# A fused layer norm, attention and gated MLP block: small steps moved from VectorE to GpSimd and the DMAs, and VectorE's exponentials taken in batches of eight

## The chip, the cores and the metric

The kernel runs on one core of one Trainium2 chip. A core has five engines, each with its own queue of instructions that it works off in order: TensorE (PE, matmuls into the PSUM memory), VectorE (DVE), ScalarE (ACT), GpSimd (POOL), and SyncE (SP), which here only issues DMAs. Engines wait for one another through semaphores. The metric is the device time of one execution in microseconds (us).

## The reference

Input x has 2,048 rows of 512. It is layer-normed, goes through attention with 32 heads of 16 that share one key and one value head, and through an MLP; the attention's output is multiplied by the silu of the MLP's output, and x is added. Cut to what matters:

```python
xn = _layernorm(x)                       # (x - m) / sqrt(v + 1e-5), rows of 512
q = (xn @ wq) as 32 heads of 16;  k = xn @ wk;  v = xn @ wv      # one k and v for all heads
p = softmax(q @ k.T * 16 ** -0.5)        # 32 x 2048 x 2048
s = (p @ v, heads side by side) @ wo
g = silu(silu(xn @ w1) @ w2)             # 512 -> 1792 -> 512
return x + s * g
```

## The kernel before

The program is written by a planner: Python code that keeps a clock for each engine, puts tasks with a cost, a priority, what they read and write and what must come first on a list per engine, and places them one by one on the engine whose clock is lowest. What comes out is a fixed order of instructions on every engine and the semaphore waits between them (`finalize`, `run_engine`). The constants at the top of the file are the costs and the rules of that order. On the chip nothing is reordered: an instruction whose input is late holds all behind it on its engine.

**Start.** x is loaded in tiles of 128 rows. For each tile VectorE takes mean and variance (lines 499 and 503), and for a group of two or four tiles the inverse root of the variance plus 1e-5 by a bit trick and two Newton steps: eight VectorE instructions on 128x2 or 128x4 numbers (lines 516 to 525), each waiting for the one before. `first = (2, 2, 4, 4, 4)` says how many tiles each group has. Then VectorE normalises the tiles (528), TensorE transposes them, and k and v are made. GpSimd clears parts of the key and value buffers in this stage (459, 461) and issues four DMAs; line 456 has it run one tiny INT64_ADD at the very start.

**Attention.** The 32 heads in four blocks of 512 rows make 32 groups `g`; two groups, `2*oi` and `2*oi + 1`, are one pair `oi`. A group has 64 slots, each a 128x512 block of scores that four matmuls write into one PSUM bank (line 898). A slot is turned into exponentials in one of two ways:

- by ScalarE's exponential, one bank or two neighbours at a time (line 1605), and then needs one product with v;
- by VectorE, which scales the scores into 16-bit integers whose bits, read as bf16, are near the exponential (line 974, into `db_sb`). Four such slots are a batch. For a batch GpSimd adds a constant to all its integers, three times with another constant (INT64_ADD, four 16-bit numbers a word, 128 x 512 words, line 1160, into `ds_sb`). The four versions, weighted in v, together are close enough to the exponential. Such a slot needs four products with v.

`pick_d` opens a batch and fills it slot by slot, `make_shifts` and `split` hand a full batch to GpSimd (`split` also puts the same work on VectorE's list, for the end of the run), and the step that starts slots (`s_step`) weighs the two ways by how much work waits for ScalarE and for VectorE. All products with v of a group add up in one bank (line 1238): 16 rows of results and 16 rows of their denominators for each quarter of 32 partitions.

**Closing a group** (`make_norm`). VectorE transposes the bank in place in 32x32 blocks (1255), takes the reciprocal of the denominators (1258) and multiplies (1260) into `otr_sb`, after which the bank is free. When both groups of a pair are done, VectorE transposes `otr_sb` into `on_sb` (1270), which the output projection reads.

**MLP and end.** Between the slots TensorE runs the MLP's products (665), ScalarE and VectorE its activations (713, 714). When four pairs of a block are closed, the output projection (`mk_w`) runs for its four row tiles, and `final` does the rest on VectorE: the product with the gate in PSUM (766) and the sum with x, which SP has loaded into `xr_sb`, into `ob_sb` (769); SP stores it (761). The last block has a tail of its own.

GpSimd and VectorE share a rule in the planner: a task with `ports=2` waits for the last such task of the other of the two engines. The shifts on GpSimd are such tasks; the evictions of line 974 are not.

Of the kernel before, what the change touches and what calls it, by code (L numbers as in the profile page):

```python
# [15 lines left out]
P = 128  # L16
# [3 lines left out]
W1_AT, SKIP = 5, 1500.0  # L20
T_ISSUE, T_SWDGE = 450.0, 1000.0
J_BASE, J_END, MIXJ = 0.073, 1.084, 3
# [4 lines left out]
T_P, T_SH, T_TR, T_AF = 600.0, 600.0, 630.0, 63.5  # L27
T_P64, DV_MIN, T_LIB = 1015.0, 40, 300.0
HOLD_PO = 374.374
RSQRT_M = float(0x5F1FFFF9)  # L30
RSQRT_C = ((-0.703952253, 0.703952253 * 2.38924456), (-0.5, 1.5))

Q_URG = 0.308
J_SLIP = 1.308
NEXT_OB, OB_SLACK = 6, 192.595
NORM_PRIO, T_DIV = 0, 264.0
A_OPEN = 5
T_MS, V_AT = 500.0, 7
# [10 lines left out]
LINE, FETCH, FED, LOOK = 256, 3684.358, 58, 68  # L49
# [3 lines left out]
NPA, NDB, NDS, NTM = 21, 5, 8, 4  # L53
MARGIN, MARGIN_END = 19, 20
WIDE, PAIR_WAIT, GRP_WAIT = 14, 47.267, 237.034
Q_LEAD = 4.233
A_HIGH, D_HIGH, SLACK = 1582.599, 1518.392, 43.301
LEAD, CROWD, FRAG, DB_LOW = 468.141, 0.617, 2.417, 1
RUN, HOLD, PRESS = 6, 1411.229, 18
ROOM = 5  # L60
START_Z, START_H, AHEAD, NEAR = 8, 9, 1.03, 17
CLOSING, URGENT, END_DV = 2, 4.336, 55
STARVED = 511.14
JLATE, JEVAC = 1.311, 1
# [250 lines left out]
def bass_recurrent_scan__grouped_kv_mqa__dense_activation_silu__prompt_kernel(  # L315
# [29 lines left out]
    with ExitStack() as es:  # L345
# [3 lines left out]
        xn_sb = sb("xn_sb", [P, 4, D], BF16)  # L349
# [14 lines left out]
        db_sb = sb("db_sb", [P, NDB, 4 * NQ], U16)  # L364
        ds_sb = sb("ds_sb", [P, NDS, 4 * NQ], U16)
        f_sb = sb("f_sb", [P, 2, NQ], FP32)
        rcp_sb = sb("rcp_sb", [P, 2, NQ // 32], FP32)
        otr_sb = sb("otr_sb", [P, 2, NQ], BF16)
# [5 lines left out]
        ob_sb = sb("ob_sb", [P, 4, D], BF16)  # L374
# [4 lines left out]
        var_sb = sb("var_sb", [P, 2, NT], FP32)  # L379
# [7 lines left out]
        zer_sb = ob_sb[:, 3, :]  # L387
# [3 lines left out]
        XB = NDS - 4  # L391

        def x_tile(t):
            return ds_sb[:, XB + t // 4, (t % 4) * NQ:(t % 4 + 1) * NQ].bitcast(BF16)

# [17 lines left out]
        def xkey(t):  # L413
            return ("Ds", XB + t // 4, t % 4)

        def ds_keys(s):
            return [("Ds", s, h) for h in range(4)]
# [6 lines left out]
        for j in range(1, 4):  # L424
            dma(SP, "x", ds_sb[:, XB + j, :].bitcast(BF16).rearrange("p (t d) -> p t d", d=D),
                xv[:, 4 * j:4 * j + 4, :], 512, ds_keys(XB + j), prio=1)
# [15 lines left out]
        pl.add(Task(DV, 550.0, lambda v: v.memset(zer_sb, 0.0), (), [("ob", 3)], 0))  # L442
# [9 lines left out]
        for j in range(K + 1):  # L452
            pl.add(Task(DV, 60.0, lambda v, j=j: v.memset(wj_sb[:, j:j + 1], 1.0 if j == 0 else SHIFT_W[j - 1]),
                        (), [("wj", j)], 2))
        l0 = pl.add(Task(PO, 60.0, lambda g: g.memset(lib_sb[:], 0), (), ["lib"], -2))
# [14 lines left out]
        for e in (1, 0):  # L470
# [16 lines left out]
        m1 = pl.add(Task(AC, 700.0, lambda a: a.activation(f_sb[:, 0, :], x_tile(1), ACT.Copy, scale=1.0 / D,  # L487
                                                          accum_out=mv_sb[:, 1, 0:1]),
                         [xkey(1)], [("F", 0), ("me", 1)], 0, gate=lambda: "scr2" in pl.lastw))
        m2 = pl.add(Task(AC, 210.0, lambda a: a.activation(scr_sb[:, 2:3], mv_sb[:, 1, 0:1], ACT.Copy, scale=-ISD),  # L490
                         [("me", 1)], ["nb"], 0, [m1]))
        pl.add(Task(AC, 700.0, lambda a: a.activation(f_sb[:, 0, :], x_tile(1), ACT.Square, scale=ISD, bias=scr_sb[:, 2:3],
                                                      accum_out=mv_sb[:, 1, 1:2]),
                    [xkey(1), "nb", ("me", 1)], [("F", 0), ("mv", 1)], 0, [m2]))
# [11 lines left out]
        first = (2, 2, 4, 4, 4)  # L506
        a = 0
        for n in first:
            b = a + n
            tiles = range(a, b)  # L510
            g = a // 4
            y, w, h = rstd_sb[:, a:b], var_sb[:, 0, a:b], var_sb[:, 1, a:b]

            def dv(fn, reads, writes, pre, ports=1):
                return pl.add(Task(DV, 66.0, fn, reads, writes, g, [pre] if pre is not None else [], ports=ports))
            t = pl.add(Task(DV, 66.0, lambda v, a=a, b=b, w=w: v.tensor_scalar(
                w, mv_sb[:, a:b, 1], LN_EPS, None, op0=ALU.add), [("mv", i) for i in tiles], [("ve", a)], g,
                [aggr[i] for i in tiles], ports=2))
            t = dv(lambda v, y=y, w=w: v.tensor_scalar(
                y.bitcast(I32), w.bitcast(I32), -0.5, RSQRT_M, op0=ALU.mult, op1=ALU.add), [("ve", a)], [("rs", a)], t, 2)  # L520
            for it, (c0, c1) in enumerate(RSQRT_C):
                t = dv(lambda v, y=y, h=h, c0=c0: v.scalar_tensor_tensor(  # L522
                    out=h, in0=y, scalar=c0, in1=y, op0=ALU.mult, op1=ALU.mult), [("rs", a)], [("vh", a)], t)
                t = dv(lambda v, w=w, h=h: v.tensor_tensor(h, h, w, ALU.mult), [("ve", a), ("vh", a)], [("vh", a)], t)  # L524
                t = dv(lambda v, y=y, h=h, c1=c1: v.scalar_tensor_tensor(
                    out=y, in0=h, scalar=c1, in1=y, op0=ALU.add, op1=ALU.mult), [("rs", a), ("vh", a)], [("rs", a)], t)
            for i in tiles:
                xn_task[i] = pl.add(Task(DV, 323.0, lambda v, i=i: v.tensor_scalar(  # L528
                    xn_sb[:, i % 4, :], x_tile(i), mv_sb[:, i, 0:1], rstd_sb[:, i:i + 1],
                    op0=ALU.subtract, op1=ALU.mult),  # L530
                    [xkey(i), ("rs", a), ("mv", i)], [("xn", i % 4)], 1 + g, [t], ports=2,
                    gate=lambda i=i: i < 4 or i - 4 in t_done))
            a = b
# [24 lines left out]
        def mk_T(tiles, bk=None):  # L558
            n, t0 = len(tiles), tiles[0]

            def rnd(b):
                def emit(pe, b=b):
                    dst = bank(b).bitcast(BF16).rearrange("p (t d) -> p t d", d=D)
                    h = None
                    for k, t in enumerate(tiles):
                        for dc in range(NDC):
                            h = pe.transpose(dst[:, k, dc * P:(dc + 1) * P], xn_sb[:, t % 4, dc * P:(dc + 1) * P], ident[:, :])
                    return h
                return emit
# [177 lines left out]
        def scaled(tt, b, r=None):  # L747
            k = tt % 2
            if r in EVR:
                ev = pl.add(Task(AC, 490.0, lambda a: a.activation(xn_sb[:, r, :], bank(b), ACT.Copy, scale=0.25),  # L750
                                 [("ps", b)], [("xn", r)], 0))
                fin_task[tt] = Task(DV, 333.0, lambda v: v.tensor_tensor(fin_sb[:, k, :], xn_sb[:, r, :], tmp_sb[:, tt % NTM, :], ALU.mult),
# [7 lines left out]
        def store(tt, t2):  # L760
            return pl.add(Task(SP, 60.0, lambda e: e.dma_start(of.rearrange("(t p) d -> p t d", p=P)[:, tt, :], ob_sb[:, tt % 4, :]),
                               [("ob", tt % 4)], [("out", tt)], 0, [t2], dma=128 * 1024, on_place=outs.append))

        def final(tt, b):
            k = tt % 2
            t1 = Task(DV, T_P, lambda v: v.scalar_tensor_tensor(
                out=bank(b), in0=bank(b), scalar=0.25, in1=tmp_sb[:, tt % NTM, :], op0=ALU.mult, op1=ALU.mult),
                [("ps", b), ("tmp", tt % NTM)], [("ps", b)], 0, [tmp_task[tt]])
            t2 = Task(DV, T_P, lambda v: v.tensor_tensor(ob_sb[:, tt % 4, :], bank(b), xr_sb[:, tt % 4, :], ALU.add),
                      [("ps", b), ("xr", tt % 4)], [("ob", tt % 4)], 0, [t1, xr_task[tt], out_task.get(tt - 4)])  # L770
# [5 lines left out]
        def add_xr(tt):  # L776
            xr_task[tt] = pl.add(Task(SP, 60.0, lambda e: e.dma_start(xr_sb[:, tt % 4, :], xv[:, tt, :]),
                                      (), [("xr", tt % 4)], 2, [fin_task[tt - 4]] if tt >= 4 else [], dma=128 * 1024))
# [3 lines left out]
        def mk_w(tt, pace):  # L782
            c, r = divmod(tt, 4)

            def consume(jb, op):
                t1, t2 = final(tt, jb.bank)
                if tt + 4 < NT:
                    add_xr(tt + 4)
                return [t1, t2]
# [151 lines left out]
        def pick_d(t):  # L941
            if st["assigned"] < 8 or any(k not in evac_kt or evac_kt[k].op is None for k in range(NKT)):
                return None
            for bt in batches:
                for k in range(4):
                    if k not in bt.slots and slot_time(bt.g, k % 2) <= t + 20:
                        return bt, k
            if any(len(bt.slots) < 4 for bt in batches):
                return None
            g = st["gD"]  # L950
            while g < NG and (nleft[g] < (MARGIN if g < NG - 1 else MARGIN_END) or min(len(left[g, i]) for i in range(2)) < 2):
# [7 lines left out]
            for k in range(2):  # L959
                if slot_time(g, k) <= t + 20:  # L960
                    bt = Job()
                    bt.g, bt.slots, bt.b, bt.P, bt.nsh, bt.left = g, {}, free[0], {}, 0, 4 * K
# [76 lines left out]
        def start_d(t, b, d):  # L1039
            bt, k = d  # L1040
            g, i = bt.g, k % 2
            if not bt.slots:
                batches.append(bt)
                db_busy[bt.b] = 1
                resv[g, 0], resv[g, 1] = 2, 2
# [63 lines left out]
        def make_shifts():  # L1109
            for bt in list(batches):  # L1110
                if len(bt.slots) < 4:
                    continue
                while bt.nsh < K - 1:
# [4 lines left out]
                    ds_busy[s] = 4  # L1118
# [10 lines left out]
        def split(bt, s, j):  # L1129
# [9 lines left out]
            def placed_dv(pop):  # L1139
# [3 lines left out]
                ready(pop, range(4))  # L1143

            def placed_po(pop):
# [4 lines left out]
                ready(pop, range(4))  # L1150

            reads = [("Db", bt.b, i) for i in range(4)]
# [93 lines left out]

        def make_norm(g):
            oi, e = divmod(g, 2)
            o3 = otr_sb[:, oi % 2, :].rearrange("p (b d) -> p b d", d=32)
# [3 lines left out]
            for h in range(parts):  # L1253
# [9 lines left out]
                    [("ps", OB), ("ps", OB, h), ("rcp", e, h)], [("otr", oi % 2, e, h)] + [("otr", oi % 2, e)] * (h == 0), NORM_PRIO,  # L1263
# [3 lines left out]
                if e == 0:  # L1267
# [3 lines left out]
                    on_sb[:, oi % NON, cols], otr_sb[:, oi % 2, cols]),  # L1271
# [209 lines left out]
        def do_tail(t, it):  # L1481
            if it[0] == "s":
# [5 lines left out]
                if part:  # L1488
                    t2 = pl.add(Task(AC, 490.0, lambda a: a.activation(ob_sb[:, tt % 4, :], bank(tb[4 + r]), ACT.Copy),
                                     [("ps", tb[4 + r])], [("ob", tt % 4)], 0, [out_task.get(tt - 4)]))  # L1490
# [17 lines left out]
        def pe_step():  # L1508
# [44 lines left out]
            if not t_done and ("ob", 3) in pl.lastw and pl.ready(PE, [("ob", 3)], [("ps", 6)]) <= t:  # L1553
                n = st["warm"] = st.get("warm", 0) + 1
                pl.tensor("F", None, T_COLD if n <= N_COLD else MM, lambda pe: pe.matmul(
                    bank(6), lhsT=zer_sb[:, 0:P], rhs=zer_sb[:, :], start=True, stop=True), [("ob", 3)], [("ps", 6)], t, n=2)
# [156 lines left out]
```

## Time and profile before

| | us |
|---|---|
| three runs | 676.65, 680.1, 683.86 (median 680.1) |
| the profiled execution | 674.7, its span 672.9 |
| TensorE / VectorE / ScalarE / GpSimd busy | 660.8 / 632.6 / 653.9 / 612.1 |
| first shift on GpSimd starts, last one ends | 43.8, 656.0 |

The span runs from the first to the last instruction; 1.8 us of the profiled execution lie outside it. Engines go by PE, DVE, ACT, POOL and SP; PEld is TensorE's loading of weights, which runs beside its matmuls; DMA-issuing instructions show as SPq or POOLq and are not counted as busy. A group's line names the source line, engine, operation, the tile written and the tile read, the shapes, the count, then busy time and the mean ns of one, and after the second bar the idle time of the engine just before these instructions and what ended it. A window's line gives start and end, length, and for each engine the busy us and the number of instructions; the last three columns are TensorE's granted clock (1.00 throughout), the busy share of the DMA engines and GB/s.

### The profile page before, as it was taken

To read this page: it belongs to the slowest core of one execution; us is meant where nothing else is said; L and a number is where in the kernel's file an instruction comes from. 1 tells how busy PE (TensorE), PEld (TensorE's weight loads), DVE (VectorE), ACT (ScalarE), POOL (GpSimd) and SP (SyncE) were. 2 spreads that over 40 slices of the span, in tenths; PEclk is the share of its full clock that TensorE was granted. 3 is DMA by queue.
4 is the path that set the end of the run, shared out by engine and by line. 5 is a ranking of instruction groups with operands and counts; after the bars stand their busy time and mean duration, and the time that the engine had idled before them with its cause. 6 is when DMAs were issued, how large, how long until landed. Compare 5 with 4: busy or idle time off the path is not lost.

```text
span 672.9 us, 47414 instructions
## 1 busy us (share of the span) xinstructions
PE 660.8 (98%) x22086; PEld 373.0 (55%) x22086; DVE 632.6 (94%) x1158; ACT 653.9 (97%) x1172; POOL 612.1 (91%) x610
## 2 busy tenths in 40 slices
PE   8999999999999999999999999999999999999996
PEld 4446656565555655555555656656656555556551
DVE  8989999999999999999999999999999999999932
ACT  6899999999999999999999999999999999999995
POOL 4049899999999999999999999999999999999990
PEclk9999999999999999999999999999999999999999
DMA  6412200000000000000000000000000001000000
GB/s 174 138 50 82 68 4 5 4 5 4 5 4 14 27 21 21 4 5 4 6 5 4 20 20 20 19 5 5 5 4 5 5 20 35 21 4 5 4 5 33
DMA packets 11782, 14.99 MB, mean 22 GB/s; under 512 B 1857, under 2 KB 10817, under 8 KB 11585
## 3 DMA queue, kind: packets, MB, share of 16 engines
q1 hardware_dynamic: 10976, 10.78, 5.4%
q8 instruction: 172, 2.82, 1.7%
q0 software_dynamic: 320, 0.92, 0.5%
q10 hardware_dynamic: 288, 0.26, 0.1%
q14 instruction: 26, 0.20, 0.1%
HBM read 8.95 MB, written 2.10 MB: 16 GB/s over the span
## 4 chain that ended last, share of the span: by engine, by line
PE 74%; ACT 20%; DVE 4%; POOL 1%; issue 0%
PE ps L898 31%; PE ps L1238 26%; ACT pa_sb L1605 19%; PE ps L665 16%; DVE stats_sb L499 1%; ACT t_sb L713 1%; DVE xn_sb L528 1%; POOL kt_sb L461 1%; PE ps L1446 0%; DVE kt_sb L611 0%; DVE xnT_sb L578 0%; DVE v_sb L639 0%; POOL v_sb L459 0%; DVE var_sb L522 0%; DVE var_sb L524 0%
## 5 line engine op out<-in xcount | busy, mean ns | idle before, releaser
L1605 ACT ACTIVATE pa_sb<-ps 128x512 bf16<-128x512 f32 (+1 forms) x1081 | 622.8, 759 | 6.9 <-PE ps L898 6.1
L1160 POOL INT64_ADD ds_sb<-db_sb x594 | 602.8, 1044 | 12.8 <-DVE db_sb L974 6.2
L898 PE MATMUL ps<-qt_sb,kt_sb 64*32 64x512 bf16 x8192 | 564.1, 379 | 0.8 <-issue 0.4
L974 DVE TENSOR_SCALAR db_sb<-ps 128x512 uint16<-128x512 f32 x792 | 493.2, 680 | 10.8 <-PE ps L898 5.9
L1238 PE MATMUL ps<-ds_sb,v_sb 64*32 64x512 bf16 x4752 | 413.6, 377 | 0.8 <-issue 0.6
L1238 PE MATMUL ps<-pa_sb,v_sb 64*32 64x512 bf16 x2512 | 330.7, 377 | 3.0 <-ACT pa_sb L1605 2.3
L898 PEld LDWEIGHTS ps<-qt_sb,kt_sb 64*32 64x32 bf16 x8192 | 197.6, 90 | 190.0 <-ACT pa_sb L1605 81.9
L1238 PE MATMUL ps<-db_sb,v_sb 64*32 64x512 bf16 x1584 | 191.6, 377 | 0.0
L1238 PEld LDWEIGHTS ps<-ds_sb,v_sb 64*32 64x32 bf16 x4752 | 166.7, 92 | 22.0 <-issue 3.4
L665 PE MATMUL ps<-w_sb,u_sb 64*32 64x512 bf16 x1792 | 140.1, 378 | 0.5 <-issue 0.5
L665 PE MATMUL ps<-xnT_sb,w_sb 64*32 64x512 bf16 x1792 | 136.3, 378 | 0.0
L1238 PEld LDWEIGHTS ps<-pa_sb,v_sb 64*32 64x32 bf16 x2512 | 101.6, 92 | 25.1 <-ACT pa_sb L1605 11.1
L1238 PEld LDWEIGHTS ps<-db_sb,v_sb 64*32 64x32 bf16 x1584 | 59.4, 92 | 5.9 <-issue 1.1
L665 PEld LDWEIGHTS ps<-w_sb,u_sb 64*32 64x32 bf16 x1792 | 48.8, 92 | 12.8 <-issue 2.6
L665 PEld LDWEIGHTS ps<-xnT_sb,w_sb 64*32 64x32 bf16 x1792 | 44.3, 91 | 16.4 <-DVE db_sb L974 2.2
L713 ACT ACTIVATE t_sb<-ps 128x512 bf16<-128x512 f32 x72 | 48.9, 679 | 0.0
L1255 DVE STREAM_TRANSPOSE ps<-ps 128x512 f32<-128x512 f32 (+1 forms) x33 | 23.3, 708 | 17.0 <-PE ps L1238 16.8
L714 DVE SCALAR_TENSOR_TENSOR u_sb<-t_sb,ps 128x512 bf16<-128x512 bf16 x56 | 37.9, 676 | 0.5 <-ACT t_sb L713 0.3
L665 PE MATMUL ps<-xnT_sb,wq_sb 64*32 64x512 bf16 x480 | 37.3, 378 | 0.0
L665 PE MATMUL ps<-wo_sb,on_sb 64*32 64x512 bf16 x384 | 29.6, 378 | 0.0
L1284 POOL DMA_DIRECT2D kt_sb<-kt_sb x4 | 2.8, 700 | 23.8 <-DVE kt_sb L611 14.6
L665 PEld LDWEIGHTS ps<-xnT_sb,wq_sb 64*32 64x32 bf16 x480 | 11.7, 91 | 4.1 <-DVE db_sb L974 0.7
(72 smaller groups left out, 181.8 us busy)
## 6 DMA issues: line engine op xcount, KB each, us to landing
xr_sb<-in_A_x_dram SPq DMA_DIRECT2D x16, 128.0 KB, 2.3
out_dram<-ob_sb SPq DMA_DIRECT2D x16, 128.0 KB, 1.7
w_sb<-in_B_w_dram SPq DMA_DIRECT2D x1, 1792.0 KB, 7.2
ds_sb<-in_A_x_dram SPq DMA_DIRECT2D x3, 512.0 KB, 7.0
w_sb<-in_B_w_dram SPq DMA_DIRECT2D x2, 512.0 KB, 4.3
kt_sb<-kt_sb POOLq DMA_DIRECT2D x4, 224.0 KB, 3.7
w_sb<-in_B_w_dram SPq DMA_DIRECT2D x2, 384.0 KB, 4.3
wq_sb<-in_A_wq_dram SPq DMA_DIRECT2D x1, 512.0 KB, 5.2
```

The lines of the kernel that those rows point to most:

```text
L461: pl.add(Task(PO, 3540.0, lambda g: g.memset(kt_sb[0:DH, 1, :, :], 0.0), [("xn", 3)], [("kt1", c) for c in range(NC)], 3, gate=lambda: all ...
L499: ts_ = pl.add(Task(DV, 593.0, lambda v, t=t: v.bn_stats(stats_sb[:, t, :], x_tile(t)), [xkey(t)], [("st", t)], 1 + j, gate=(lambda j=j: S ...
L528: xn_task[i] = pl.add(Task(DV, 323.0, lambda v, i=i: v.tensor_scalar(xn_sb[:, i % 4, :], x_tile(i), mv_sb[:, i, 0:1], rstd_sb[:, i:i + 1], ...
L665: h = pe.matmul(bank(b)[32 * j:32 * (j + 1), :], lhsT=lhs(k, rows, 32 * j, 32), rhs=rhs(k, rows), start=first, stop=last, tile_position=(r ...
L713: t1 = Task(AC, T_AF + 0.8333 * NQ, lambda a: a.activation(t_sb[:, k, :], bank(b), ACT.Tanh, scale=scale), [("ps", b)], [("t", k)], 0)
L714: t2 = Task(DV, T_P, lambda v: v.scalar_tensor_tensor(out=dst, in0=t_sb[:, k, :], scalar=1.0, in1=bank(b), op0=ALU.add, op1=ALU.mult), [(" ...
L898: h = pe.matmul(bank(b)[32 * j:32 * j + 32, :], lhsT=kt_sb[r0:r0 + 64, g % 2, i, k0:k0 + 32], rhs=qt_sb[r0:r0 + 64, g // 2 % NQR, :], star ...
L974: bt.P[k] = pl.add(Task(DV, T_P, lambda v: v.tensor_scalar(db_sb[:, bt.b, k * NQ:(k + 1) * NQ], bank(b), 128.0 * LOG2E, 128.0 * (SHIFT_BET ...
L1160: whole["po"].append(pl.add(Task(PO, T_P64, lambda g: g.int64_add(ds_sb[:, s, :].bitcast(U64), db_sb[:, bt.b, :].bitcast(U64), words), rea ...
L1238: h = pe.matmul(bank(OB)[q:q + 32, :], lhsT=lhs[rows], rhs=rhs[rows], start=s0, stop=s1, tile_position=(64 * l, q), skip_group_check=True)
L1255: t1 = pl.add(Task(DV, (T_TR - 60.0) / parts + 60.0, lambda v, cols=cols: v.transpose(bank(OB)[:, cols], bank(OB)[:, cols]), [("ps", OB)], ...
L1605: op = pl.place(AC, 0.8333 * NQ * n + T_AF, lambda a: a.activation(pa_sb[:, s * NQ:(s + n) * NQ].rearrange("p (b n) -> p b n", n=NQ), ps3[ ...
```

## The change

Four things change, and with them nearly all of the planner's constants.

1. *Inverse roots.* The bit trick and the Newton steps go. VectorE adds 1e-5 to the variances, and GpSimd raises them to the power -0.5 in one instruction (`tensor_tensor` with `ALU.pow`). The groups are four tiles each.
2. *Closing a group.* For 15 of the 16 pairs `moved_norm` takes the place of the transposes. VectorE copies the bank to SBUF and frees it. DMAs on SP's queue bring the denominators into a 128x16 shape; after the second group of the pair VectorE takes both reciprocals in one instruction; four DMAs move the second group's rows beside the first's; two DMAs write the reciprocals to a small DRAM tensor and one reads them back so that each partition holds the ones of its row. GpSimd multiplies (128x512, fp32) into `on_sb`. No transposes are needed, since rows stay rows. The last pair is closed as before.
3. *Residual.* For 12 of the 16 row tiles VectorE's product goes to `fin_sb`, and GpSimd adds x into `xr_sb`, from which SP stores. `ob_sb` is gone; a tile of `xr_sb` is loaded again only after its store.
4. *Batches.* `BS = 8`: a batch has eight slots, a shift is one INT64_ADD of 128 x 1,024 words. There are three buffers of eight for the integers (five of four before) and four of eight for the shifts (eight of four before), and 24 instead of 21 slots for ScalarE's results. A batch is opened in a group only while 26 slots are left (19 before).

```diff
-T_P, T_SH, T_TR, T_AF = 600.0, 600.0, 630.0, 63.5
-T_P64, DV_MIN, T_LIB = 1015.0, 40, 300.0
+T_P, T_SH, T_TR, T_AF = 600.0, 1130.0, 630.0, 63.5
+T_P64, DV_MIN, T_LIB = 1812.0, 40, 300.0
...
+FIN_PRIO, ON_PRIO = 6.803, 3
+T_DMA, T_GT, T_REC = 3200.0, 1300.0, 252.0
+FIRST, T_POW = (4, 4, 4, 4), 350.0
...
-NPA, NDB, NDS, NTM = 21, 5, 8, 4
-MARGIN, MARGIN_END = 19, 20
+BS = 8
+NPA, NDB, NDS, NTM = 24, 3, 4, 4
+MARGIN, MARGIN_END = 26, 27
...
-            t = dv(lambda v, y=y, w=w: v.tensor_scalar(
-                y.bitcast(I32), w.bitcast(I32), -0.5, RSQRT_M, op0=ALU.mult, op1=ALU.add), [("ve", a)], [("rs", a)], t, 2)
-            for it, (c0, c1) in enumerate(RSQRT_C):
...
+            t = pl.add(Task(PO, T_POW, lambda v, a=a, b=b: v.tensor_tensor(
+                rstd_sb[:, a:b], var_sb[:, a:b], mhalf_sb[:, a:b], ALU.pow), [("ve", a), "mhalf"], [("rs", a)], g, [t], ports=2))
...
-        def final(tt, b):
+        def final(tt, b, po=False):
             k = tt % 2
+            if po:
+                t1 = Task(DV, T_P, lambda v: v.scalar_tensor_tensor(
+                    out=fin_sb[:, k, :], in0=bank(b), scalar=0.25, in1=tmp_sb[:, tt % NTM, :], op0=ALU.mult, op1=ALU.mult),
+                    [("ps", b), ("tmp", tt % NTM)], [("fin", k)], 0, [tmp_task[tt], out_task.get(tt - 2)])
+                t2 = Task(PO, T_GT, lambda g: g.tensor_tensor(xr_sb[:, tt % 4, :], fin_sb[:, k, :], xr_sb[:, tt % 4, :], ALU.add),
+                          [("fin", k), ("xr", tt % 4)], [("xr", tt % 4)], FIN_PRIO, [t1, xr_task[tt]], ports=2)
...
+        def shift_dma(name, size, out_, in_, reads, writes, preds, prio=-1):
+            task = pl.add(Task(SP, 60.0, lambda e: e.dma_start(out_, in_), reads, writes, prio, preds, dma=size * 1024))
+            task.ring = name
+            return task
+
+        def moved_norm(g):
+            oi, e = divmod(g, 2)
+            OB, k = ob[g], oi % 2
+            okeys = [("xn", 2 * k), ("xn", 2 * k + 1)]
+            dst, keys = (e_sb[:, :], ["eb"]) if e else (o_sb[:, k, :], okeys)
+            ev = norm[g] = pl.add(Task(DV, T_P, lambda v: v.tensor_copy(dst, bank(OB)), [("ps", OB)], keys, NORM_PRIO,
+                                       on_place=lambda op: pool_free.append(OB)))
+            nb = NQ // 32
+            norm["d", g] = shift_dma("den%d" % e, 300, den_sb[:, e, :], dst[DH:P:32], keys, [("den", e)], [ev])
+            if e == 0:
+                return
+            rec = pl.add(Task(DV, T_REC, lambda v: v.reciprocal(inv_sb[:, :, :], den_sb[:, :, :]), [("den", 0), ("den", 1)], ["inv"], 3,
+                              [norm["d", g - 1], norm["d", g]]))
+            put = [shift_dma("put%d" % q, 32, o_sb[32 * q + DH:32 * q + 2 * DH, k, :], e_sb[32 * q:32 * q + DH, :], ["eb", ("den", 0)] + okeys,
+                             [("moved", k, q)], [ev, norm["d", g - 1]]) for q in range(4)]
+            rows = [shift_dma("row%d" % a, 200, in_dram(a * NQ, [[2 * NQ, 4], [16, 32], [1, 16]]), inv_sb[:, a, :], ["inv"], [("row", a)], [rec])
+                    for a in range(2)]
+            fill = shift_dma("fill", 256, rr_sb[:, :], in_dram(0, [[NQ, 8], [0, DH], [1, NQ]]), [("row", 0), ("row", 1)], ["rr"], rows)
+            cc = oi // NOC - NON // NOC
+            t2_task[oi] = pl.add(Task(PO, T_GT, lambda p: p.tensor_tensor(on_sb[:, oi % NON, :], o_sb[:, k, :], rr_sb[:, :], ALU.mult),
+                                      okeys + ["rr"] + [("moved", k, q) for q in range(4)], [("on", oi % NON)], ON_PRIO, put + [fill], ports=2,
...
         def make_norm(g):
             oi, e = divmod(g, 2)
-            o3 = otr_sb[:, oi % 2, :].rearrange("p (b d) -> p b d", d=32)
+            if oi < NO - 1:
+                return moved_norm(g)
+            o3 = otr_tile(oi % 2).rearrange("p (b d) -> p b d", d=32)
```

## The prediction

> **What bounds the kernel now.** I read the page's first part, then the windows, then the costliest groups.
>
> ```profile
> PE 660.8 (98%) x22086; PEld 373.0 (55%) x22086; DVE 632.6 (94%) x1158; ACT 653.9 (97%) x1172; POOL 612.1 (91%) x610
> ```
>
> All engines look full, so I go by stage. In the windows (columns: busy us and count of PE, PEld, DVE, ACT, POOL):
>
> ```profile
> 20.00:40.00 20.00, 18.31 (x492) 9.70 (x484) 17.24 (x49) 17.67 (x27) 1.66 (x3) 1.00 0.26 92
> 150.00:200.00 50.00, 49.99 (x1732) 27.39 (x1720) 49.09 (x85) 49.73 (x91) 50.00 (x50) 1.00 0.02 5
> 550.00:600.00 50.00, 49.70 (x1716) 28.16 (x1701) 49.07 (x85) 49.44 (x91) 50.00 (x50) 1.00 0.07 20
> ```
>
> GpSimd is idle until about 44 us and then has no gap until 656. Four engines share the score slots of the softmax: 2,048 (8,192 matmuls of line 898, four each), of which 792 go to VectorE and GpSimd and 1,256 to ScalarE.
>
> ```profile
> L1605 ACT ACTIVATE pa_sb<-ps 128x512 bf16<-128x512 f32 (+1 forms) x1081 | 622.8, 759 | 6.9 <-PE ps L898 6.1
> L1160 POOL INT64_ADD ds_sb<-db_sb x594 | 602.8, 1044 | 12.8 <-DVE db_sb L974 6.2
> L974 DVE TENSOR_SCALAR db_sb<-ps 128x512 uint16<-128x512 f32 x792 | 493.2, 680 | 10.8 <-PE ps L898 5.9
> ```
>
> A slot costs ScalarE 622.8/1,256 = 0.496 us, or VectorE 493.2/792 = 0.62 plus GpSimd 602.8/792 = 0.761. TensorE pays three more products for a VectorE slot, six matmuls; eight run side by side each 0.2145 us (the start distance in the timeline), so 0.16 us. From 100 to 640 us it issues 18,656 matmuls where 540 us hold 20,140: 93%. ScalarE and GpSimd bind together, VectorE and TensorE just behind. Whatever holds GpSimd holds the run, because the order on every engine is fixed when the program is written.
>
> **The change, part by part,** without the last point below.
>
> *Batches of eight.* 594 shifts of 512 words become 297 of 1,024. The one-word INT64_ADD below takes 0.230 us, the normal one 1.044: 0.814 is per word, so 1.858 for the double, less the 0.03 by which neighbours overlap (602.8/594 = 1.015): **1.83**. Bounds: two times the part per word, 1.63, and no saving, 2.03. GpSimd needs 297 x 1.83 = 543.5, 59 us less. The first batch waits for four more evictions, 4 x 0.62 = 2.5 us later.
>
> *Head groups and residual.* VectorE loses, per pair of groups, two transposes, reciprocals and products and the second transpose. One closing, in time order:
>
> ```profile
> 309.63 0.73 DVE L1255 STREAM_TRANSPOSE ps<-ps 128x512 f32<-128x512 f32 x1
> ...
> 311.01 0.25 DVE L1258 RECIPROCAL rcp_sb<-ps 128x16 f32<-128x16 f32 x1
> ...
> 311.72 0.41 DVE L1260 TENSOR_TENSOR otr_sb<-ps,rcp_sb 128x256 bf16<-128x256 f32 x1
> ...
> 312.64 0.70 DVE L1270 STREAM_TRANSPOSE on_sb<-otr_sb 128x512 bf16<-128x512 bf16 x1
> ```
>
> From start to next start these hold 0.68, 0.16, 0.32 and 0.62 us, so 2 x 1.16 + 0.62 = 2.9 a pair and 44 for 15. In their place come two plain copies (0.62 as line 974) and one reciprocal of 32 (0.2): 1.45 a pair, 22. Twelve residual adds go, 12 x 0.62 = 7.4. VectorE gains **29 us**. GpSimd gets 15 products and 12 adds of 128x512. No row has a two-input operation there: a memset of 128x512 (0.52 us) is below, two passes of INT64_ADD (2.03) above; two fp32 operands are the bytes of one INT64_ADD, so 1.0 to 1.5, and I take **1.2**: 32 us. The Trainium skill (GPSIMD Engine Reference, Elementwise) gives 4.5 us for an add of 2,048, which I estimate at 1.15 here; the sum would move by 1 us.
>
> *The DMAs.* Nine a pair, 135 on SP's queue, at 0.34 to 0.51 us of issue: 4 us in each 40 of a queue that mostly waits. They stand among the residual loads and stores, whose next need is 10 us off. The path of a product (denominators, reciprocal, rows to DRAM, refill) is three landings of 1.7 to 2.3 us and the issues, about 8 us; only the output projection, a head group later, needs it. If it were late, GpSimd would stand at the product with its shifts behind.
>
> *Inverse roots.* Seven VectorE instructions 0.2 apart leave the path of each row group, one on GpSimd (0.23 to 1.0) and two hand-overs come: 1.4 us against 0.6 to 1.4, so at most 0.8 us gained in each of three groups, about none in the first, which now waits for four tiles.
>
> *What GpSimd and VectorE can do with it.* GpSimd has 59 - 32 = 27 us: at 3 x 1.83/8 = 0.686 a slot that is **39 slots**, for which VectorE pays 24 of its 29 us. ScalarE then has 39 x 0.496 = 19 us less, TensorE 39 x 0.16 = 6 more. Its densest 10 us are full (373 matmuls), but the mean is 345, so I let two thirds of the 19 through: -13, -1 net in the prologue. **Span 659.**
>
> *What stands between the operations on GpSimd.* The instructions of line 456, the program's first INT64_ADD (duration min/median/max, start):
>
> ```profile
> L456 POOLq MODIFY_POOL_CONFIG  x2: 11/11/11, 0.9 to 0.9; - x2
> L456 POOL INT64_ADD lib_sb<-lib_sb x1: 230/230/230, 1.0 to 1.0; - x1
> ```
>
> Two configuration instructions stand ahead of the first INT64_ADD and nowhere else; afterwards GpSimd runs only memsets, DMA issues and 594 more INT64_ADDs, so nothing had to be set up again. The change puts TENSOR_TENSOR between them. My reading, which this trace doesn't show, is that it needs another set-up and undoes that of INT64_ADD: two swaps per TENSOR_TENSOR that stands alone between shifts, 27 x 2 = **54**, and two around the powers. Price by rows: below, 0.09 us, as here from the pair to the add (the set-up may have been there from the run before). If code is fetched, the nearest row is a small load from DRAM:
>
> ```profile
> wk_sb<-in_A_wk_dram SPq DMA_DIRECT2D x1, 16.0 KB, 3.0
> ...
> wv_sb<-in_A_wv_dram SPq DMA_DIRECT2D x1, 16.0 KB, 4.2
> ```
>
> One trip is 3.0 us; two instructions are two trips, **6.0**; above, 2 x 4.2 = 8.4. I take 6.0, for a reload of other code is nearer to a load than to a reload of the same. Nothing hides it: GpSimd has no gap, and behind the swap its shifts queue, which TensorE's products wait for. 54 x 6.0 = 324 us; before the first power (its queue gets there at 4.4 us, after two memsets) 6 us put the first tiles at 10.9 instead of 7.3, +3.6, and the swap back lies in the idle time before the first shift. 659 + 324 + 3.6 = 987.
>
> The Trainium skill (GPSIMD Engine Reference, Instruction dispatch) says that GpSimd's kernels are loadable and that a freshly loaded one costs about 6 us at its first call, without a visible instruction. By it the 54 would be 321 us; by this trace's 0.09 us they would be 5. This rule speaks against the change, and no row here shows its 6 us.
>
> **Against the time.** The profiled run took 674.7 us at a span of 672.9, and the median of the three is 680.1, 0.8% more. (987 + 1.8) x 1.008 = **997**.
>
> **The rivals.** (a) *It pays*: TENSOR_TENSOR needs no swap, or a swap is as cheap as here. (659 + 1.8) x 1.008 = **666**; if TensorE lets all 19 us through and shifts take 1.63 (VectorE then limits to 47 slots, 23 us), 655. For it: the 0.09 us. Against: TensorE at 93% already. (b) *TensorE gets no denser*: 680, within 1%. The chain of waits speaks for it, most steps being matmuls:
>
> ```profile
> PE 74%; ACT 20%; DVE 4%; POOL 1%; issue 0%
> ```
>
> (c) *GpSimd stands at the products for their DMAs*, no swaps: its 27 us over 15 products break even at 1.8 us of waiting each; at 4 us it loses 33, which is 48 slots and 24 us for ScalarE: (697 + 1.8) x 1.008 = 704, slower. With shifts at 1.92 us or more (543.5 + 27 = 297 x 1.92) the gain is gone as well.
>
> **How the numbers follow.** Swaps that cost: 0.60. I put this above one half because the pair shows that INT64_ADD needs a set-up, and the fixed order gives no cover; the 0.09 us keep it from being more. Its own range: one trip, 54 x 3.0 = 162, gives 832; 8.4 us give 1,130. (a) 0.28, (b) 0.06, (c) 0.06. So faster by over 1% 0.28, within 1% (about what three runs between 676.65 and 683.86 can tell) 0.06, slower 0.66. Cases of both signs count, so the range goes from 658, which leaves out the lower end of (a), to 1,110, which leaves out the upper end of the first: about 0.8 is left inside.
>
> **What will show it.** Swaps: MODIFY_POOL_CONFIG dozens of times, GpSimd idle some 6 us after each, 12 us around every TENSOR_TENSOR, TensorE and ScalarE idle with it. (a): one pair, GpSimd full, some 830 of line 974, TensorE over 95% in the middle. (c): GpSimd idle before its products, released by a DMA. Step by step: INT64_ADD at 1.86 us, TENSOR_TENSOR near 1.2, copies at 0.68. I am wrong if the configuration stands there but takes no time, or if one set-up serves both operations.

## The result, and the profile after

| | before | after |
|---|---|---|
| median of the runs, us | 680.08 | 1046.9 |
| all runs, us | 676.65 to 683.86 | 1045.72 to 1051.66 |
| profiled execution / its span, us | 674.7 / 672.9 | 1045.72 / 1043.8 |
| GpSimd busy, us | 612.1 | 600.9 |
| TensorE busy, us / mean granted clock | 660.8 / 1.000 | 730.9 / 0.841 |

The ratio is 1.539 (95% interval 1.531 to 1.547): the changed kernel is 54% slower. The forecast was 997 us, and the case that it held likeliest came, 50 us dearer. The range of 658 to 1,110 us held cases of both signs, so that the time lies inside it says little; what counts is which case it was.

The page of the changed kernel, first part (busy time and share of the span), then the chain of work that ended last:

```profile
PE 730.9 (70%) x22084; PEld 382.8 (37%) x22084; DVE 615.6 (59%) x1051; ACT 667.6 (64%) x1159; POOL 600.9 (58%) x344
...
issue 34%; POOL 31%; PE 28%; DVE 4%; ACT 3%; DMA 0%; POOLq 0%; ACTq 0%; DVEq 0%
```

The windows that were shown of before, in the same columns:

```profile
150.00:200.00 50.00, 38.34 (x1288) 19.28 (x1284) 36.84 (x62) 36.99 (x66) 36.80 (x20) 0.90 0.04 12
550.00:600.00 50.00, 37.64 (x1220) 21.95 (x1208) 34.57 (x57) 35.17 (x64) 28.92 (x17) 0.86 0.05 12
```

No engine is full any more: in 50 us each has 29 to 38 us of work, GpSimd too. Before, 74% of the chain was matmuls; now a third of it is "issue", time in which an engine waits for nothing that the profile shows, and another third is GpSimd. Whose issue time that is, the waits of GpSimd say (what was waited for, total us, times, longest):

```profile
POOL ds_sb L1175 <- issue: 158.5, 27, 6.1
POOL on_sb L1286 <- issue: 106.5, 15, 7.6
POOL xr_sb L776 <- issue: 77.6, 11, 7.4
...
POOL rstd_sb L531 <- issue: 10.2, 1, 10.2
POOL xr_sb L776 <- DVE db_sb L989: 7.1, 1, 7.1
```

Every one of the 15 products (line 1286) and 12 residual sums (776) has a gap of some 7 us ahead of it, and so has the first shift behind it (1175), of some 6 us. (One of the twelve sums is put down to VectorE; its length is that of the others.) The sum is 106.5 + 77.6 + 7.1 + 158.5 = 349.7 us at the 54 places, 6.5 us each. In the timeline of GpSimd one such place looks so (start, length, instruction, in brackets the idle time before it):

```profile
90.47 3.78 POOL L1175 INT64_ADD ds_sb<-db_sb  x2
101.40 1.27 POOL L1286 TENSOR_TENSOR on_sb<-o_sb,rr_sb 128x512 bf16<-128x512 f32 x1 [7.15 <-issue]
108.65 3.76 POOL L1175 INT64_ADD ds_sb<-db_sb  x2 [5.98 <-issue]
```

A product of 1.27 us takes GpSimd out of the run for 14.4. At the head of each gap stands a pair of MODIFY_POOL_CONFIG, in the trace's rows for the three lines (count, duration in ns min/median/max, first and last start):

```profile
L1286 POOLq MODIFY_POOL_CONFIG  x30: 1/16/25, 94.2 to 997.2; - x30
```

```profile
L776 POOLq MODIFY_POOL_CONFIG  x24: 1/12/38, 288.0 to 963.6; - x24
```

```profile
L1175 POOLq MODIFY_POOL_CONFIG  x56: 1/1/37, 49.9 to 1005.5; - x56
```

They are 15, 12 and 28 pairs; with one for the first power and the one at the very start, 57 in place of 1. The instructions themselves take some ns, the time is behind them. The other engines wait for GpSimd, in the groups by line:

```profile
L1650 ACT ACTIVATE pa_sb<-ps 128x512 bf16<-128x512 f32 (+1 forms) x1068 | 633.0, 724 | 328.9 <-PE ps L913 299.7
L989 DVE TENSOR_SCALAR db_sb<-ps 128x512 uint16<-128x512 f32 x792 | 499.4, 683 | 360.3 <-POOL ds_sb L1175 291.1
L1175 POOL INT64_ADD ds_sb<-db_sb x296 | 554.6, 1890 | 200.4 <-issue 158.5
...
L1253 PE MATMUL ps<-ds_sb,v_sb 64*32 64x512 bf16 x4752 | 397.2, 412 | 147.1 <-POOL ds_sb L1175 146.8
...
L1286 POOL TENSOR_TENSOR on_sb<-o_sb,rr_sb 128x512 bf16<-128x512 f32 x15 | 18.8, 1255 | 106.5 <-issue 106.5
...
L776 POOL TENSOR_TENSOR xr_sb<-fin_sb,xr_sb 128x512 bf16<-128x512 bf16 x12 | 13.7, 1141 | 84.7 <-issue 77.6
```

The columns behind the bar are busy us and mean ns of one, then the idle time before them. VectorE has as many slots as before, 792, and takes about as long for them (499 us, 493 before), but stands idle for 360 us ahead of them, 291 of it waiting for the shifts; ScalarE waits for TensorE's scores (300 us), and TensorE for the shifts. The whole line of engines stands still with GpSimd.

### The profile page after: what moved, and what is told of

It is laid out like the page before. It is cut to its first block, busy times and chain, and to the rows that moved or that the text cites. A ratio compares the mean times of both kernels' runs of the same rounds, so it can differ in the third digit from the quotient of the medians.

```text
span 1043.8 us, 47229 instructions
## 1 busy us (share of the span) xinstructions
PE 730.9 (70%) x22084; PEld 382.8 (37%) x22084; DVE 615.6 (59%) x1051; ACT 667.6 (64%) x1159; POOL 600.9 (58%) x344
## 4 chain that ended last, share of the span: by engine, by line
issue 34%; POOL 31%; PE 28%; DVE 4%; ACT 3%; DMA 0%; POOLq 0%; ACTq 0%; DVEq 0%
POOL ds_sb L1175 27%; PE ps L913 12%; PE ps L1253 9%; PE ps L671 6%; ACT pa_sb L1650 2%; DVE db_sb L989 2%; POOL on_sb L1286 2%; POOL xr_sb L776 1%; DVE stats_sb L515 1%; POOL rstd_sb L531 0%; DVE o_sb L534 0%; DMA ds_sb<-in_A_x_dram 0%; PE ps L573 0%; PE ps L1491 0%; DVE kt_sb L617 0%
## 5 line engine op out<-in xcount | busy, mean ns | idle before, releaser
L1175 POOL INT64_ADD ds_sb<-db_sb x296 | 554.6, 1890 | 200.4 <-issue 158.5
L913 PE MATMUL ps<-qt_sb,kt_sb 64*32 64x512 bf16 x8192 | 614.3, 405 | 56.3 <-DVE db_sb L989 55.4
L1253 PE MATMUL ps<-ds_sb,v_sb 64*32 64x512 bf16 x4752 | 397.2, 412 | 147.1 <-POOL ds_sb L1175 146.8
L1253 PE MATMUL ps<-pa_sb,v_sb 64*32 64x512 bf16 x2512 | 269.4, 394 | 20.5 <-POOL ds_sb L1175 19.0
L1253 PEld LDWEIGHTS ps<-ds_sb,v_sb 64*32 64x32 bf16 x4752 | 142.4, 97 | 207.2 <-POOL ds_sb L1175 163.4
L1253 PE MATMUL ps<-db_sb,v_sb 64*32 64x512 bf16 x1584 | 173.8, 412 | 25.7 <-POOL ds_sb L1175 25.7
L671 PE MATMUL ps<-w_sb,u_sb 64*32 64x512 bf16 x1792 | 141.0, 394 | 11.3 <-DVE db_sb L989 11.3
L1253 PEld LDWEIGHTS ps<-pa_sb,v_sb 64*32 64x32 bf16 x2512 | 85.3, 95 | 51.8 <-POOL ds_sb L1175 21.0
L1286 POOL TENSOR_TENSOR on_sb<-o_sb,rr_sb 128x512 bf16<-128x512 f32 x15 | 18.8, 1255 | 106.5 <-issue 106.5
L776 POOL TENSOR_TENSOR xr_sb<-fin_sb,xr_sb 128x512 bf16<-128x512 bf16 x12 | 13.7, 1141 | 84.7 <-issue 77.6
L720 DVE SCALAR_TENSOR_TENSOR tmp_sb<-t_sb,ps 128x512 bf16<-128x512 bf16 x16 | 10.9, 681 | 12.3 <-ACT t_sb L719 12.1
```

The source lines that it names most:

```text
L671: h = pe.matmul(bank(b)[32 * j:32 * (j + 1), :], lhsT=lhs(k, rows, 32 * j, 32), rhs=rhs(k, rows), start=first, stop=last, tile_position=(r ...
L720: t2 = Task(DV, T_P, lambda v: v.scalar_tensor_tensor(out=dst, in0=t_sb[:, k, :], scalar=1.0, in1=bank(b), op0=ALU.add, op1=ALU.mult), [(" ...
L776: t2 = Task(PO, T_GT, lambda g: g.tensor_tensor(xr_sb[:, tt % 4, :], fin_sb[:, k, :], xr_sb[:, tt % 4, :], ALU.add), [("fin", k), ("xr", t ...
L913: h = pe.matmul(bank(b)[32 * j:32 * j + 32, :], lhsT=kt_sb[r0:r0 + 64, g % 2, i, k0:k0 + 32], rhs=qt_sb[r0:r0 + 64, g // 2 % NQR, :], star ...
L1175: whole["po"].append(pl.add(Task(PO, T_P64, lambda g: g.int64_add(ds_sb[:, s, :].bitcast(U64), db_sb[:, bt.b, :].bitcast(U64), words), rea ...
L1253: h = pe.matmul(bank(OB)[q:q + 32, :], lhsT=lhs[rows], rhs=rhs[rows], start=s0, stop=s1, tile_position=(64 * l, q), skip_group_check=True)
```

## The experiments

The theory is the prediction's: INT64_ADD and TENSOR_TENSOR need different set-ups on GpSimd, each change from one to the other costs some 6 us, and nothing hides it. The rivals: the loss comes from the new order itself (nine DMAs for a pair of head groups, batches of eight with three larger buffers), from the large operands, or from a slower TensorE clock. What is also open is whether the change would have paid without the swaps. Ratios are to the kernel before as it was timed beside each run (677.48, 682.58 or 679.78 us), so that the runs are compared by them.

### The same order without the 27 operations

The edit, cut to the two bodies:

```diff
-lambda p: p.tensor_tensor(on_sb[:, oi % NON, :], o_sb[:, k, :], rr_sb[:, :], ALU.mult)
+lambda p: p.int64_add(on_sb[:, oi % NON, :].bitcast(U64), wq_sb[:, oi % NDC, :].bitcast(U64), 0)
...
-lambda g: g.tensor_tensor(xr_sb[:, tt % 4, :], fin_sb[:, k, :], xr_sb[:, tt % 4, :], ALU.add)
+lambda g: g.int64_add(xr_sb[:, tt % 4, :].bitcast(U64), xr_sb[:, tt % 4, :].bitcast(U64), 0)
```

The planner's order, the waits and the DMAs stay as they are on every engine.

> The changed kernel with the same order of instructions, waits and DMAs on every engine; only the bodies of the 15 products and 12 residual sums on GpSimd are INT64_ADDs of 128 words (the product and the sum are left out: the tile gets other numbers of the same kind). The four powers stay. Theory, the swaps: about 350 us of idle time of GpSimd at these 27 places go, and some 20 us of work, and TensorE sets the end again: 655 to 695 us, configuration pairs 57 down to 3, granted clock back near 1.00. Rival, the order itself (nine DMAs a pair, batches of eight with three buffers, residual tiles loaded after their stores): VectorE's 291 us of waiting for shifts stay in good part, 750 us or more. Rival, a slower clock with a cause of its own: TensorE's 731 us stay, at least 735.

Measured: 692.67 us against 677.48, ratio 1.021 (1.017 to 1.025); span 690.7, that is 353.1 below the changed kernel. Its page:

```profile
PE 667.3 (97%) x22084; PEld 380.6 (55%) x22084; DVE 609.4 (88%) x1051; ACT 657.0 (95%) x1159; POOL 578.1 (84%) x344
...
L989 DVE TENSOR_SCALAR db_sb<-ps 128x512 uint16<-128x512 f32 x792 | 495.0, 681 | 36.7 <-PE ps L913 17.1
```

VectorE's 360 us of idle time are 37, the granted clock is 0.992, and TensorE is full. On GpSimd the 349.7 us of gaps have gone and 22.8 of work with them (600.9 to 578.1); 19 of these come back as other waits of its shifts (60.9 us, against 41.9 beside the gaps), and 353 show in the span. So the loss lies at these 27 operations, and neither the order nor a clock of its own makes it. That it is the gaps and not the size of the operations, the tiny ones below show. Of the DMAs GpSimd waits for one, once:

```profile
POOL on_sb L1286 <- DMA rr_sb<-inv_dram: 0.5, 1, 0.5
```

So the rival of products that wait for their DMAs falls too; in this run no swap covers the transfers.

### The powers taken out as well

The edit, cut to the body:

```diff
-lambda v, a=a, b=b: v.tensor_tensor(
-    rstd_sb[:, a:b], var_sb[:, a:b], mhalf_sb[:, a:b], ALU.pow)
+lambda v, a=a, b=b: v.int64_add(
+    rstd_sb[:, a:b].bitcast(U64), var_sb[:, a:b].bitcast(U64), 0)
```

> As the run without the 27, and the four powers too are INT64_ADDs (of 2 words; the inverse root is left out, the variance is used for it). Theory: the two swaps around the powers lie on the path of the start, the first shift on GpSimd comes at 44 to 47 us instead of 55.9, and the time is 8 to 12 us lower than with the powers. Rival, they are hidden behind the loads of x and the weights: within 2 us of it.

Measured: 681.47 us, ratio 1.0063 (1.004 to 1.009), 11.2 us below the run with the powers. The start of GpSimd with the powers, in its timeline:

```profile
14.63 1.05 POOL L531 TENSOR_TENSOR rstd_sb<-var_sb,mhalf_sb 128x4 f32<-128x4 f32 x1 [10.30 <-issue]
...
41.17 1.03 POOL L531 TENSOR_TENSOR rstd_sb<-var_sb,mhalf_sb 128x4 f32<-128x4 f32 x1
...
55.87 3.77 POOL L1175 INT64_ADD ds_sb<-db_sb  x2 [6.25 <-DVE db_sb L989]
```

and without them:

```profile
6.44 0.19 POOL L531 INT64_ADD rstd_sb<-var_sb  x1 [2.09 <-DVE var_sb L528]
...
29.92 0.20 POOL L531 INT64_ADD rstd_sb<-var_sb  x1
...
44.38 5.62 POOL L1175 INT64_ADD ds_sb<-db_sb  x3 [6.29 <-DVE db_sb L989]
```

The first power comes 8.2 us later than an operation without a swap would; by the fourth the delay is 11.3, in good part since each power takes 1.04 us in place of 0.20 and the next row group waits for it. The swap back is hidden: both kernels wait 6.3 us there, and in both the first shift starts 5.6 us behind the first eviction of line 989. The first shift is 11.5 us late, and the time nearly as much.

This kernel has no swap but still isn't faster than before. Its shifts wait 59 us, most of them for TensorE:

```profile
L1175 POOL INT64_ADD ds_sb<-db_sb x296 | 554.7, 1892 | 58.7 <-PE ps L1253 29.4
```

That comes back below.

### Tiny operations in the kernel before

One multiplication of 128x4 numbers ahead of every 21st shift, 27 of them:

```diff
+        def shift64(g, dst, src, words):
+            n_shift[0] += 1
+            if n_shift[0] in range(20, 580, 21):
+                for i in range(1):
+                    g.tensor_tensor(tiny_sb[:, 4 * i + 4:4 * i + 8], tiny_sb[:, 0:4], tiny_sb[:, 0:4], ALU.mult)
+            h = g.int64_add(dst, src, words)
+            return h
```

> The kernel before, with one multiplication of 128x4 fp32 (TENSOR_TENSOR, result unused) on GpSimd ahead of every 21st shift, 27 of them, and nothing else changed. Theory, a swap there and a swap back each time, 12.5 us in all, and nothing hides them: 27 x 12.5 = 338, so 1,000 to 1,030 us. Rival, the loss needs the large operands, the DMAs or the batches of eight: at most 27 x 0.3 = 8 us, 675 to 690. Rival, eight shift buffers and five batches give cover: each swap pair costs half, 830 to 870.

Measured: 1032.65 us, ratio 1.522 (1.517 to 1.526), 355 us more, or 13.1 for each of the 27; that is 3 us above the range of the theory, which had 12.5 for each. The waits of its GpSimd:

```profile
POOL tiny_sb L392 <- issue: 186.0, 26, 7.8
POOL ds_sb L393 <- issue: 160.6, 27, 6.3
...
POOL tiny_sb L392 <- PE ps L909: 7.0, 1, 7.0
```

That is 193.0 / 27 = 7.1 us into TENSOR_TENSOR and 160.6 / 27 = 5.9 back, the same as around the large products, for an operation of 0.19 us and 2 KB. With 27 x 0.19 the sum is 359, and 355 show in the time: eight shift buffers and five batches give no cover at all. Almost the whole loss of the change is had by one line that computes nothing.

What GpSimd does in a gap the trace doesn't show. The DMA queues that it counts carry nothing for it. The page of this run with its 54 swaps:

```profile
DMA packets 11782, 14.99 MB, mean 15 GB/s; under 512 B 1856, under 2 KB 10816, under 8 KB 11584
```

The kernel before, with no swap, also has 11,782 packets and 14.99 MB.

Three in a row in 9 places (`range(40, 600, 63)`, `range(3)`):

> The kernel before, with the same 27 multiplications in 9 places, three in a row. Theory, the price is per change of operation, not per instruction: 9 x 12.7 = 114, 785 to 805 us. Rival, each TENSOR_TENSOR pays: as with 27 places, 1,000 to 1,030.

Measured: 797.01 us, ratio 1.174 (1.170 to 1.178), 119.5 us more, 13.3 for each place. In the timeline:

```profile
94.29 0.50 POOL L392 TENSOR_TENSOR tiny_sb<-tiny_sb 128x4 f32<-128x4 f32 x3 [6.73 <-DVE otr_sb L1271]
100.78 6.11 POOL L393 INT64_ADD ds_sb<-db_sb  x6 [6.00 <-issue]
```

Three operations share one pair of gaps. The price is per change of operation, not per instruction. (The first gap is put down to VectorE in this row; its length gives it away.)

### What the set-up outlives

Before and after, the program's first INT64_ADD starts 0.1 us behind its pair of MODIFY_POOL_CONFIG. One tiny multiplication behind the last shift, in the kernel before:

```diff
             h = g.int64_add(dst, src, words)
+            if n_shift[0] == 594:
+                g.tensor_tensor(tiny_sb[:, 4:8], tiny_sb[:, 0:4], tiny_sb[:, 0:4], ALU.mult)
```

> The kernel before, with one multiplication of 128x4 fp32 on GpSimd behind its last shift and nothing else changed. Theory, the set-up outlives an execution, and the free pair at the start of both kernels (0.09 us) finds that of INT64_ADD left from the execution ahead of it: now the first INT64_ADD starts 5.5 to 7.5 us behind its pair, at 6.5 to 8.5 us instead of 1.0, and the time is 0 to 6 us longer, since the swap at the end lies beside the tail. Rival, each execution starts with INT64_ADD's set-up in place, or its first set-up is cheap: still 0.1 us.

Measured (one execution): 683.78 us against 682.58. The first INT64_ADD in GpSimd's timeline:

```profile
7.40 0.18 POOL L469 INT64_ADD lib_sb<-lib_sb  x1 [6.53 <-issue]
```

The pair stands at 1.1 us, and the first INT64_ADD now comes 6.3 us behind it; the multiplication at the end starts at 672.3 us, behind a gap of 7.1. The version with 27 tiny operations has the same start, with the same tile cleared ahead of it, but its last operation is an INT64_ADD: there the pair stands at 0.9 us and the first INT64_ADD at 1.0. So the free pair of the kernel before was free because the execution ahead had left INT64_ADD's set-up in place. This rests on one execution, but the step from 0.1 to 6.3 us is far from any noise. The 0.09 us, the prediction's lower bound, was the price of no swap.

### The 27 operations on VectorE

```diff
-            t2_task[oi] = pl.add(Task(PO, T_GT, lambda p: p.tensor_tensor(on_sb[:, oi % NON, :], o_sb[:, k, :], rr_sb[:, :], ALU.mult),
+            t2_task[oi] = pl.add(Task(DV, T_P, lambda p: p.tensor_tensor(on_sb[:, oi % NON, :], o_sb[:, k, :], rr_sb[:, :], ALU.mult),
...
-                t2 = Task(PO, T_GT, lambda g: g.tensor_tensor(xr_sb[:, tt % 4, :], fin_sb[:, k, :], xr_sb[:, tt % 4, :], ALU.add),
+                t2 = Task(DV, 333.0, lambda g: g.tensor_tensor(xr_sb[:, tt % 4, :], fin_sb[:, k, :], xr_sb[:, tt % 4, :], ALU.add),
```

> The changed kernel with the 15 products and 12 residual sums as VectorE instructions, all else of the change kept (copies, nine DMAs a pair, batches of eight, powers on GpSimd), the order written anew by the planner. Theory: without the swaps in the middle the loss is gone, the swaps around the powers still cost some 11 us, VectorE pays about 15 x 0.7 + 12 x 0.4 = 15 us of work that TensorE's bound hides in part: 685 to 705 us. Rival, moving the rows by DMAs is itself worth something: under 677 us.

Measured: 697.71 us, ratio 1.021 (1.015 to 1.028), 15 us more than the kernel before beside it. Nothing of the computation is left out here, and 352 of the 367 us are gone. Some 11 of the 15 that remain are what the powers cost in the run above; the first one waits 10.1 us here too. Closing head groups by DMAs shows no gain here.

### Batches of eight alone

`moved_norm` is not called, `final` gets no third argument, the inverse roots are those of before; BS stays 8, and the planner's constants are those of the change.

> The kernel before with batches of eight alone (and the changed kernel's constants of the planner): inverse roots, closing of the groups and residual as before, no other operation than INT64_ADD on GpSimd. GpSimd's work falls by some 50 us. Theory, TensorE sets the time and shifts are no bound: 668 to 685 us, within 1% of before. Rival, as the prediction's sum had it, GpSimd's free time lets ScalarE do less and the time falls by 13 us or more: at most 665 us.

Measured: 682.58 us, ratio 0.999 (0.995 to 1.003). GpSimd's busy time falls from 612.1 to 560.6, and it stands idle instead:

```profile
L1186 POOL INT64_ADD ds_sb<-db_sb x294 | 551.3, 1899 | 76.1 <-DVE db_sb L1000 33.8
```

VectorE takes 792 slots as before, and TensorE is at 98% as before. GpSimd's time was not what the run was short of.

### 832 slots in place of 792

The kernel without products, sums and powers, with four of the planner's limits changed (cut):

```diff
-MARGIN, MARGIN_END = 26, 27
+MARGIN, MARGIN_END = 16, 27
...
-A_HIGH, D_HIGH, SLACK = 1370.087, 863.23, 45.072
+A_HIGH, D_HIGH, SLACK = 1000.0, 2000.0, -300.0
```

> The kernel without any other operation on GpSimd than INT64_ADD (products, residual sums and inverse roots left out as there), with four limits of the planner set so that VectorE and GpSimd take 832 slots instead of 792, about the 39 that the prediction gave them. By the prediction's sum ScalarE has 40 x 0.496 = 20 us less, TensorE 6 us more work but less waiting, and the time falls by 13 us against the run with 792: 664 to 670 us. Rival, TensorE is the bound and has no gaps to give: its 6 us and any disorder come on top, 685 to 700 us.

Measured: 691.79 us, ratio 1.019 (1.015 to 1.022), against 1.006 with 792 slots: 1.25% or 8 us more. Its page:

```profile
PE 676.6 (98%) x22324; PEld 386.8 (56%) x22324; DVE 628.1 (91%) x1090; ACT 648.0 (94%) x1232; POOL 604.8 (88%) x360
...
PE 95%; DVE 2%; issue 1%; DMA 1%; SPq 0%; ACT 0%; DVEq 0%
...
L1650 ACT ACTIVATE pa_sb<-ps 128x512 bf16<-128x512 f32 (+1 forms) x1141 | 614.3, 684 | 25.2 <-PE ps L913 14.7
```

ScalarE's line is 8.7 us shorter than with 792 slots (623.0 there), not 20: it does two banks at a time 75 times in place of 188, so each of its slots costs more, 614.3/1,216 = 0.505 us. It waits 25 us, mostly for TensorE. TensorE has 240 matmuls more, six a slot as the prediction counted, and 95% of the chain. From 100 to 600 us (busy us and count of PE, PEld, DVE, ACT, POOL) with 832 slots:

```profile
100.00:600.00 500.00, 498.00 (x16902) 284.92 (x16890) 472.00 (x783) 482.68 (x932) 474.64 (x271) 1.00 0.07 20
```

and with 792:

```profile
100.00:600.00 500.00, 495.36 (x16932) 290.16 (x16927) 466.91 (x768) 493.31 (x879) 463.31 (x266) 1.00 0.08 20
```

ScalarE has work for 10.6 us less in this stretch, and TensorE takes no more matmuls, 16,902 against 16,932. In this order freeing ScalarE makes TensorE no denser. Of the 8 us, 40 x 0.16 = 6 are TensorE's own extra work; the rest may be the disorder of an order that nobody tuned. Whether a tuned order with 832 slots would do better wasn't run.

### Batches of eight, the order searched

Batches of eight alone, with 15 of the planner's limits and priorities searched for the shortest plan, for instance:

```diff
-WIDE, PAIR_WAIT, GRP_WAIT = 14, 23.547, 345.594
+WIDE, PAIR_WAIT, GRP_WAIT = 14, 8.514, 345.594
...
-A_HIGH, D_HIGH, SLACK = 1370.087, 863.23, 45.072
+A_HIGH, D_HIGH, SLACK = 1370.087, 885.982, 25.938
```

> Batches of eight alone, as before, with 17 of the planner's limits and priorities searched for the shortest plan (2.4 us shorter than that of the run before it). If plan and chip agree: 0.3 to 0.7% under the kernel before. If TensorE's bound is all that counts: within 0.3% of it.

(The edit changes 15 constants, not 17.) Measured: 676.35 us against 679.78, ratio 0.996 (0.994 to 0.998). It is 0.4% faster than the kernel before, the lowest ratio of all that ran, and a small thing. Against batches of eight alone, which have a ratio of 0.999, only the order is new; it gives VectorE 800 slots, and TensorE takes 17,240 matmuls from 100 to 600 us, where batches of eight alone have 16,882 and the kernel before 17,280.

## Why the prediction was right, and where it was off

**The swaps, right.** INT64_ADD and TENSOR_TENSOR do need different set-ups, both ways, at each of the 27 places: 54 swaps as counted. A swap into TENSOR_TENSOR takes 7.1 us and one back 5.9, mean 6.5 where 6.0 was taken. The sum is 350 us for a forecast of 324. That nothing hides them was right (353 us of span for 350 of gaps and 23 of work; 355 of time for 359 in the tiny version).

How the 6.0 was reached is another matter. It stood for two loads from DRAM of 3.0 us, one for each configuration instruction. By the profile's count the run with 54 swaps moves no DMA packet more than the kernel before, and nothing else here shows two trips. That the size came near is luck as far as the runs can tell; what takes the 6 to 7 us stays open. The Trainium skill (GPSIMD Engine Reference, Instruction dispatch) gives some 6 us, measured as 5.95, for the first call to a freshly loaded kernel, with no visible instruction. The way back, 5.9, agrees; the way in is 1.2 us dearer, and the one beside the loads at the start, 10.3, dearer still.

**The lower bound, misread.** The chance of 0.28 for "it pays" rested on the 0.09 us between the pair and the first INT64_ADD. The prediction said itself that the set-up might have been there from the run before; the run with a multiplication at the end shows that it was. The row proved nothing for a cheap swap, and the swaps should have had more than 0.60.

**The start, too low.** Forecast were 3.6 us, measured 11. The swap into the first power took 10.3 us in place of 6, of which 2.1 would have been waiting anyway: 8.2. The power itself takes 1.04 us, just past the upper bound of 1.0, so each row group gains nothing against VectorE's 1.4 and its hand-overs. That the swap back lies in idle time was right.

**What the kernel would be without swaps, wrong in sign.** The forecast was a span of 659 against 672.9, by 39 more slots. The swap-free order, which leaves out the products, sums and powers, has 677.8, with 792 slots and 59 us of idle time of GpSimd ahead of its shifts, 43 of them waiting for TensorE. Two steps failed. "For which VectorE pays": the planner's order doesn't hand out more slots because GpSimd is faster; the trace after has 792 as before. And "I let two thirds of the 19 through": TensorE's 345 matmuls in 10 us, against 373 at its densest, were taken as room. With the 40 slots given, none of it came through, and the time rose. The 39 x 0.496 = 19 us for ScalarE were too many as well: a slot less saved it 8.7/40 = 0.22 us there, since it took more banks singly. Rival (b), TensorE gets no denser, fits the runs without swaps: from 100 to 600 us none of the four without any swap takes more matmuls than the 17,280 of the kernel before. The chain of waits with its 74% of matmuls had spoken for it. What keeps TensorE at 345 is not settled here, nor is it shown that no order could use the slots.

**The sum.** From 988.8 for the profiled execution to 1,045.7 are 57 us: 26 from the size of the swaps, 8 from the start, 19 from the span without them (677.8 in place of 659). The 4 that remain weren't traced; the bodies of the 27 operations, shorter in the run that gives the 677.8, may be a part of them.

**Rows that held.** A shift of 1,024 words is 1.89 us, start to start 1.87 (1.83 forecast, bounds 1.63 and 2.03). A product takes 1.26 and a sum 1.14 us where 1.2 was taken. Rival (c), GpSimd waiting for a product's DMAs, didn't show: 0.5 us in all without the 27 operations, 1.1 without the powers too.

## What to carry to other kernels

Before an operation of a new kind goes on GpSimd, count how often the order of its queue would change between kinds, and price each change at 6 to 7 us: three such operations in a row cost hardly more than one, and one alone costs 13 us, however small it is. This was measured for INT64_ADD and TENSOR_TENSOR. Not every operation has such a price: MEMSETs and DMA issues stand between the four powers of the changed kernel, and only the first power has a pair ahead of it. A pair of MODIFY_POOL_CONFIG ahead of the first instruction of a kind is the sign to look for, and a short gap behind it proves nothing if the execution ahead ended with the same kind. Work taken off an engine is a gain only if the engine that sets the end gets less of it: here GpSimd was freed of 51 us in one run and the time didn't move.

## What was not expected

- The set-up outlives an execution: the last kind of operation in one decides what the first costs in the next (0.1 or 6.3 us).
- A swap into TENSOR_TENSOR is dearer than one into INT64_ADD (7.1 and 5.9 us), for large and tiny operations alike; beside the loads of the start it took 10.3.
- TensorE's mean granted clock is lower the more idle time a run has: 0.841 in the changed kernel, 0.847 with 27 tiny operations, 0.931 with 9 places, 0.992 and more with none in the middle. The matmuls of the scores take 405 ns there in place of 379, and TensorE is busy for 731 us; but the gaps and the work of the 27 operations account for the time lost, so the slower clock seems to have lain in time that was lost already. No run changes the clock alone.
